# The last 64 rows of the first batch's k and v by one transfer over 128 partitions, and one more spin of TensorE

## The chip, the core and the metric

The kernel runs on one core of a Trainium2 chip. The core has five engines that run their own instruction streams side by side: TensorE (PE, matrix products; PEld is its weight load), VectorE (DVE), ScalarE (ACT), GpSimdE (POOL) and SyncE (SP, which issues most transfers). Transfers between the chip's memory (HBM) and the core's own memory (SBUF, 128 partitions) run on 16 DMA engines, which two queues feed here: one filled by SP, one by ACT. The metric is the device time of one execution in microseconds, lower is better.

## The reference

```python
a = exp(phi - max(phi, axis=2)); a = a / (sum(a, axis=2) + 1e-09)     # phi: 8 batches, 8 heads, 576, 32
k_m = einsum('bhsm,bhsd->bhmd', a, k); v_m = einsum('bhsm,bhsd->bhmd', a, v)
scores = matmul(q, k_m^T) / sqrt(64); scores -= max(scores)
attn = exp(scores) / (sum(exp(scores)) + 1e-09)
x = matmul(attn, v_m)            # laid out as 4608 tokens by 512
h = maximum(x @ w_in, 0); out = (h * h) @ w_out                        # 512 -> 2048 -> 512
```

Everything is in float32. For each batch and head, 576 rows of k and v are reduced to 32 "memories" with the weights exp(phi), queries attend to these 32 memories, and a two-layer feed-forward network with a squared ReLU follows.

## The kernel before, in words

The 576 rows of a batch are five chunks of at most 128 partitions: four full ones and a last one of 64 rows. The eight heads are two groups of four (`qd` 0 and 1). The chunks of phi for both groups stand in `e_sb` (128 partitions, 5 chunks, 256 columns); k and v of one group and chunk are 512 float32 in a partition (4 heads, 64 of k and 64 of v).

The first batch is done before anything else can start, by an order written out by hand (the string `order` that the loop at L1381 follows). Its steps on the path:

- `load_phi` (L161) issues the three transfers of phi: the short last chunk from ACT's queue (L168), the others from SP's (L174, L176).
- `first_kv` (L1302) loads k and v: group 0 from ACT's queue into `u_hi3`, `u_lo3` and `u_hi4`, group 1 from SP's into `wp2` and `wp3`, two chunks by transfer (L1316) and the 64 rows of the last chunk by a transfer of their own (L1320).
- `fetch` (L565) loads the weights `w_in` and `w_out`, 512 KB by transfer, behind these on SP's queue. They come as coded words that ACT, DVE and POOL decode (`decode`, L584 to L609).
- `exp_phi`: DVE takes the maximum over the five chunks (L186, L189), PE and DVE bring it to all rows (L206 to L214), DVE subtracts it (L224), ACT takes the exponential (L225).
- `memories` (L302): PE multiplies each chunk of exponentials with a column of ones (`add`, L318) and with k and v (`product`, L327). Ahead of the products of chunk 2 PE does two products with the identity (L341). DVE and ACT copy the result to `mem` (L417).
- `attend` (L453): scores (L439), their maximum, exponential (L478) and sums. While nothing else is there for it, PE runs `spin`: products with the identity whose result nobody reads (L159).
- `make_u`: PE multiplies the decoded `w_in` (`w_sb`) with the memories (L439, into `ps_m`), and ACT copies this to `u_hi` (L550). The feed-forward products of the first batch (L687, L708) follow.

What sets the order around the change: every engine runs its instructions in program order. Each transfer signals one of eight semaphores, taken in turn by both queues together, and the issue of a transfer waits for the landing of the one that stands eight before it. So at most eight transfers are in flight. ACT's stream has the decode of the first half of `w_in` (L584, L587, L590) between the first exponentials (L225) and its half of the copy of the memories (L417), and the decode of the second half between that copy and the exponentials of the scores (L478). Behind the first batch an instruction plan of fixed places feeds PE with products for the other seven batches.

Of the kernel before, what the change touches and what calls it, by code (L numbers as in the profile page):

```python
# [9 lines left out]
F32 = mybir.dt.float32  # L10
# [17 lines left out]
def attn_moe_kernel(ctx: ExitStack, tc: tile.TileContext, qT, kv, phi, w_in, w_out, outT):  # L28
# [12 lines left out]
    nc = tc.nc  # L41
    ctx.enter_context(tc.manual_schedule())

    B, NQ, S = kv.shape[:3]
    P = 128
# [3 lines left out]
    D = 64  # L49
    M = 32  # L50
# [6 lines left out]
    CW = 2 * D + 2  # L57
    NCH = (S + P - 1) // P
# [9 lines left out]
    def rows(c):  # L68
        return min(P, S - c * P)

    const = ctx.enter_context(tc.tile_pool(name="const", bufs=1))
# [37 lines left out]
    e_sb = const.tile([P, NCH, NQ * P], F32, name="e_sb")  # L109
    kvb = [const.tile([P, 4, CW], F32, name=f"kvb{i}") for i in range(NCH)]  # L110

    def fill(c, t):
        if rows(c) < P:
            nc.gpsimd.memset(t[rows(c):], 0.0)
        if t.shape[-1] == CW:
            nc.gpsimd.memset(t[:rows(c), :, 2 * D:], 1.0)

    def fill_all():
        for c in range(NCH):
            fill(c, kvb[c])  # L120
            if rows(c) < P:
                nc.gpsimd.memset(e_sb[rows(c):, c], 0.0)

    ones = const.tile([P, CW - 2 * D], F32, name="ones")
    nc.gpsimd.memset(ones, 1.0)
# [35 lines left out]
    def load_phi(b, nc_q=nc.sync):  # L161
        nfull = S // P
        assert b == 0 or ("products", b - 1) in ready
        n = nfull if b else nfull // 2
        x = phi[b, :nfull * P].rearrange("(c p) x -> p c x", p=P)
        def short():
            if nfull < NCH:
                nc_q.dma_start(out=e_sb[:rows(nfull), nfull], in_=phi[b, nfull * P:])  # L168
                if b >= 3:
                    nc_q.dma_start(out=e_sb[P - rows(nfull):, nfull], in_=phi[b, nfull * P:])  # L170

        if not b:
            short()
        nc.sync.dma_start(out=e_sb[:, :n], in_=x[:, :n])  # L174
        if not b:
            nc.sync.dma_start(out=e_sb[:, n:nfull], in_=x[:, n:])  # L176
        if b:
            short()
        return [e_sb[:P if b >= 3 else rows(c), c] for c in range(NCH)]

    def chunk_max(e):

# [119 lines left out]
    def memories(b, e, kvs, mem):  # L302
# [9 lines left out]
        accs = [bank(ps, qd if not b or two else 0)[:, (qd if b and not two else 0) * CW:] for qd in range(NQ)]  # L312
        sums = [(ps_h.tile([P, 512], F32, name="h") if qd else tp) if not b else accs[qd][:, 2 * D:] for qd in range(NQ)]

        def add(qd, c):
            n = kvs[qd][c].shape[0]
            for j in range(4):
                nc.tensor.matmul(  # L318
                    sums[qd][M * j:M * (j + 1), :CW - 2 * D], e[c][:n, qd * P + M * j:qd * P + M * (j + 1)], ones[:n],
                    start=(c == 0), stop=(c == len(kvs[qd]) - 1),  # L320
                )

        def product(qd, c):
            y = kvs[qd][c]
            n, w = y.shape[0], y.shape[-1]
            for j in range(4):
                nc.tensor.matmul(  # L327
                    accs[qd][M * j:M * (j + 1), :w],
                    e[c][:n, qd * P + M * j:qd * P + M * (j + 1)],
                    y[:, j, :], start=(c == 0), stop=(c == len(kvs[qd]) - 1),  # L330
                )

# [26 lines left out]
        if two:  # L359
            n = rows(NCH - 1)  # L360
            for j in range(4):
                for qd in range(NQ):
                    y = kvs[qd][-1] if qd else kvs[qd][-1][:n]
# [22 lines left out]
        for qd in turns:  # L386
            x = accs[qd][:, :2 * D].rearrange("p (x d) -> p x d", x=2)[:, :, None, :].broadcast_to([P, 2, 2, D])
# [9 lines left out]
        if b > 2:  # L397
            done_ps(ps)
            for j in range(4):
                if j == 2 or j and b > JOIN:  # L400
                    yield
                for k in range(2):
                    for x in range(2):
                        at = M * (2 * (j % 2) + k)
# [42 lines left out]
            y = rhs[pr // NQ][hs, pr % NQ]  # L447
            nc.tensor.matmul(out[M * pr:M * (pr + 1), :y.shape[-1]], mem[hs, x, pr], y, start=True, stop=True)  # L448

    spins = [2, 3]  # L450
    on_gpsimd = {(0, 0): (), (0, 1): (), (1, 0): (), (1, 1): (2,), (2, 0): (0, 1, 2), (2, 1): (0,)}

    def attend(b, t, q, mem, new_a):  # L453
# [761 lines left out]
    def task_phi(b):  # L1215
        state[b]["phi"] = load_phi(b)
# [81 lines left out]

    st = state[0]
    kvs = [None] * NQ  # L1300

    def first_kv(qd):  # L1302

        if qd:
            x = [const.tile([P, 2, 2, 4, 2 * D], F32, name=f"wp{k}") for k in (2, 3)]
            rooms = [x[0][:, 0], x[0][:, 1], x[1][:, 0]]
        else:
            rooms = [const.tile([P, 2, 4, 2 * D], F32, name=n) for n in ("u_hi3", "u_lo3", "u_hi4")]
        queues = ((nc.scalar, nc.scalar, nc.scalar), (nc.sync, nc.sync, nc.sync))[qd]
        got = []  # L1310
        for t, nc_q in zip(rooms, queues):
            c = len(got)
            n = min(2, S // P - c)
            if n:
                x = kv[0, qd, c * P:(c + n) * P].rearrange("(c p) h x -> p c h x", p=P)
                nc_q.dma_start(out=t[:, :n], in_=x)  # L1316
                got += [t[:, k] for k in range(n)]
            else:
                fill(c, t[:, 0])
                nc_q.dma_start(out=t[:rows(c), 0], in_=kv[0, qd, c * P:])  # L1320
                got.append(t[:, 0])
        kvs[qd] = got

    def first_phi():
        st["phi"] = load_phi(0, nc.scalar)
        fill_all()
# [231 lines left out]
    for k, step in enumerate(steps):  # L1558
        i, b, t, f = step
# [5 lines left out]
        n = f * P // FC  # L1565
# [53 lines left out]
    for j in range(-1, LAST + 1):  # L1619
# [31 lines left out]
        if new:  # L1651
            ffn1_product(u1, j + 1, 1, True)
            ffn1_product(z, j + 1, 2, True)
            x = from_z(j + 1, 2, *(("g_hi", 3) if old else ("r", 2)))
# [19 lines left out]
    n = (B - JOIN) * REST  # L1674
# [23 lines left out]
    last = banks["h"] + [banks["z"], banks["m"]]  # L1698
# [55 lines left out]
```

## Time and profile before

| | |
|---|---|
| median of 3 runs | 696.65 us (696.21 to 697.31) |
| the profiled execution's own time | 695.58 us |
| its span, first to last instruction | 693.5 us |
| PE busy | 682.5 us (98% of the span) |
| DVE, ACT, POOL busy | 480.5, 439.7, 345.0 us |
| bytes moved by transfers | 89.85 MB, mean 130 GB/s |

A profile lists every instruction's start and duration on each engine and every transfer's issue and landing. The share of busy time is a mean over the program; what the first 60 us are bound by is not what the rest is bound by. The granted clock of TensorE is given as a share of 2.4 GHz, so 0.50 is 1.2 GHz. The profiled execution took 2.1 us more than its span, and 1.07 us less than the median of the three runs.

### The profile page before, as it was taken

The page shows a single profiled execution, that of the slowest core. Times are in us where ns is not written, and L with a number is a line of the kernel's source. Part 1 is how long each engine was busy: PE and PEld are TensorE (multiplying, and loading weights), DVE is VectorE, ACT ScalarE, POOL GpSimd, SP SyncE. Part 2 cuts the span into 40 slices and gives each one's busy share as a digit, 9 for nine tenths or more (in the row PEclk, how much of TensorE's full clock was granted, in tenths as well). Part 3 has the DMA queues.
Part 4 walks back from the last instruction along what each step waited for, and adds up shares of the span by engine and source line. Part 5 has one row for each costly group of instructions (what it writes and reads, how often), then busy time and mean ns, then how long its engine had stood idle before and what let it go on. Part 6 is the DMA issues. An engine that isn't in the chain of part 4 may idle for free.

```text
span 693.5 us, 14173 instructions
## 1 busy us (share of the span) xinstructions
PE 682.5 (98%) x5102; PEld 573.8 (83%) x5102; DVE 480.5 (69%) x1132; ACT 439.7 (63%) x1193; POOL 345.0 (50%) x528
## 2 busy tenths in 40 slices
PE   8899999999999999999999999999999999999997
PEld 4367889899998888888888888888888888888897
DVE  3879849455787976788678976788677765564432
ACT  3867798876456675566666665667666575655531
POOL 2200343343367675747575675757585567554200
PEclk9999999999999999999999999999999999999999
DMA  9997352509424642082336243355106110400102
GB/s 304 353 376 263 126 163 60 187 2 268 139 62 147 219 129 100 25 251 86 97 116 210 88 130 122 118 180 151 64 18 211 62 60 4 166 17 1 57 6 46
DMA packets 67846, 89.85 MB, mean 130 GB/s; under 512 B 6848, under 2 KB 56064, under 8 KB 64192
## 3 DMA queue, kind: packets, MB, share of 16 engines
q1 hardware_dynamic: 65888, 87.41, 38.9%
q10 hardware_dynamic: 1888, 1.54, 0.7%
q8 instruction: 40, 0.66, 0.4%
q14 instruction: 30, 0.25, 0.1%
HBM read 75.30 MB, written 13.63 MB: 128 GB/s over the span
## 4 chain that ended last, share of the span: by engine, by line
PE 91%; DMA 6%; DVE 2%; ACT 1%; issue 0%; ACTq 0%; SPq 0%; DVEq 0%
PE acc L1112 39%; PE h L1136 11%; PE acc L716 9%; PE z L1136 8%; PE h L687 6%; PE acc L708 4%; PE h L1704 2%; DMA e_sb<-in_phi 1%; DMA u_lo<-in_kv 1%; PE z L448 1%; PE m L1704 1%; PE z L1704 1%; PE ps_m L439 1%; PE m L327 1%; PE m L448 1%; DMA wp<-in_w_in 1%
## 5 line engine op out<-in xcount | busy, mean ns | idle before, releaser
L1112 PE MATMUL acc<-u_hi,wp 128*128 128x512 f32 x576 | 153.8, 396 | 0.0
L1112 PE MATMUL acc<-u_lo,wp 128*128 128x512 f32 x576 | 140.0, 392 | 0.0
L1112 PEld LDWEIGHTS acc<-u_hi,wp 128*128 128x128 f32 x576 | 101.2, 188 | 25.9 <-issue 11.0
L1112 PEld LDWEIGHTS acc<-u_lo,wp 128*128 128x128 f32 x576 | 105.5, 188 | 20.5
L1160 POOL TENSOR_TENSOR u_hi<-g_lo,u_hi 128x288 fp32r<-128x288 f32 (+1 forms) x76 | 59.2, 779 | 64.1 <-ACT g_lo L1157 44.2
L700 POOL TENSOR_TENSOR g_lo<-g,g_hi 128x288 fp32r<-128x288 f32 x48 | 43.2, 901 | 78.1 <-ACT g_hi L698 51.4
L1016 POOL TENSOR_TENSOR u_lo<-low,u_hi 128x128 fp32r<-128x128 f32 (+1 forms) x116 | 73.2, 636 | 16.6 <-ACT u_hi L1015 16.0
L1015 ACT CAST u_hi<-low 128x256 fp32r<-128x256 f32 (+1 forms) x160 | 52.8, 347 | 23.0 <-POOL low L1027 19.0
L1152 DVE CUSTOM_DVE_ANT_0 g_hi<-h,g_hi 128x288 f32<-128x288 f32 x95 | 42.7, 449 | 24.5 <-ACT g_hi L1183 24.2
L716 PE MATMUL acc<-g_hi,wp 128*128 128x288 f32 x360 | 58.8, 297 | 0.0
L1183 ACT COPY g_hi<-z 128x288 f32<-128x288 f32 x72 | 28.6, 398 | 44.2 <-PE z L1136 36.6
L716 PEld LDWEIGHTS acc<-g_hi,wp 128*128 128x128 f32 x360 | 51.0, 188 | 4.4 <-ACT r L689 1.7
L1155 ACT ACTIVATE u_hi<-g_hi 128x224 fp32r<-128x224 f32 x95 | 39.0, 410 | 21.7 <-DVE g_hi L1152 21.7
L1177 DVE TENSOR_TENSOR g_lo<-h,g 128x288 f32<-128x288 f32 x48 | 21.5, 448 | 34.9 <-ACT g L1173 33.8
L689 ACT ACTIVATE r<-h 128x288 f32<-128x288 f32 x64 | 26.0, 406 | 27.9 <-PE h L687 27.6
L1136 PE MATMUL z<-a_hi,u_hi 128*128 128x288 f32 x120 | 35.3, 294 | 0.0
L1136 PE MATMUL h<-a_lo,u_hi 128*128 128x288 f32 x120 | 34.6, 295 | 0.0
L716 PE MATMUL acc<-g_lo,wp 128*128 128x288 f32 x180 | 34.6, 295 | 0.0
L1178 POOL TENSOR_TENSOR u_lo<-g_lo,u_lo 128x288 fp32r<-128x288 f32 x30 | 25.1, 835 | 18.5 <-DVE g_lo L1177 18.5
L708 PE MATMUL acc<-g_hi,wp 128*128 128x288 f32 x128 | 33.7, 410 | 0.5 <-ACT a_hi L508 0.5
L1136 PE MATMUL h<-w_sb,u_hi 128*128 128x288 f32 x120 | 34.1, 296 | 0.0
L687 PE MATMUL h<-a_hi,u_hi 128*128 128x288 f32 x128 | 30.8, 327 | 1.0 <-DVE a_hi L493 1.0
(374 smaller groups left out, 1778.1 us busy)
## 6 DMA issues: line engine op xcount, KB each, us to landing
w_sb<-w_f SPq DMA_DIRECT2D x24, 1024.0 KB, 5.5
wp<-in_w_in SPq DMA_DIRECT2D x16, 512.0 KB, 8.4
wp<-in_w_out SPq DMA_DIRECT2D x16, 512.0 KB, 7.9
kvb<-in_kv SPq DMA_DIRECT2D x28, 256.0 KB, 7.1
tmp<-in_kv SPq DMA_DIRECT2D x24, 256.0 KB, 5.8
q_sb<-in_q SPq DMA_DIRECT2D x15, 384.0 KB, 4.7
w_f<-w_sb SPq DMA_DIRECT2D x4, 1024.0 KB, 6.4
e_sb<-in_phi SPq DMA_DIRECT2D x7, 512.0 KB, 4.2
```

The lines of the kernel that those rows point to most:

```text
L687: nc.tensor.matmul(h[:, :T], u[:, qd, fs], x[:, qd], start=(i == 0), stop=(i == len(todo) - 1))
L700: nc.gpsimd.tensor_tensor(out=g_lo, in0=g, in1=g_hi.bitcast(F32), op=ALU.subtract)
L708: nc.tensor.matmul(acc[e][:, :T], wo[f][:, e * P:(e + 1) * P], g_hi, start=first, stop=last)
L716: nc.tensor.matmul(acc[e][:, :T], wo[f][:, w, e * P:(e + 1) * P], x, start=first and x is g_hi and w == 0, stop=last and x is g_lo,)
L1015: nc.scalar.copy(hi[:, k], x)
L1016: by(name, p).tensor_tensor(out=lo[:, k], in0=x, in1=hi[:, k].bitcast(F32), op=ALU.subtract)
L1112: nc.tensor.matmul(late_accs[e], wo[f][:, w, e * P:(e + 1) * P], x, start=f == 0 and first, stop=f == NFT - 1 and last,)
L1136: nc.tensor.matmul(out[:, :T], u[:, lhs], a, start=first and not n, stop=n == 2, skip_group_check=not first)
L1152: nc.vector._custom_dve(TENSOR_ADD_SAT, out=x, in0=u[:, :T], in1=x, s0=float("inf"), s1=0.0)
L1155: nc.scalar.square(g_hi, x[:, :n])
L1160: by(f"c{k}", p).tensor_tensor(out=g_lo, in0=g[:, :n], in1=g_hi.bitcast(F32), op=ALU.subtract)
L1183: (nc.vector.tensor_copy if late_on[f"z{k}"] >> pairs[j][1] & 1 else nc.scalar.copy)(x, banks["z"][:, :T])
```

## The change

The 64 rows of the last chunk of k and v of the first batch are now loaded for both groups by one transfer into 128 partitions: group 0 in partitions 0 to 63, group 1 in 64 to 127 (`last`, a part of `wp3`). So that the weights of the products stand in the same partitions, the 64 rows of phi are loaded twice, into the lower and the upper half, by one transfer whose source is repeated. The products of the last chunk take 64 partitions each in place of 128, of which 64 had been zeros; the three memsets that wrote those zeros are gone, and the one that batch 1 needs in `e_sb` is done later. The second number of `spins` goes from 3 to 4.

```diff
     def fill_all():
         for c in range(NCH):
             fill(c, kvb[c])
-            if rows(c) < P:
-                nc.gpsimd.memset(e_sb[rows(c):, c], 0.0)
...
         def short():
-            if nfull < NCH:
+            if nfull < NCH and not b:
+                n = rows(nfull)
+                y = phi[b:b + 1, nfull * P:].broadcast_to([P // n, n, NQ * P])
+                nc_q.dma_start(out=e_sb[:, nfull], in_=y)
+            elif nfull < NCH:
+                if b == 1:
+                    nc.gpsimd.memset(e_sb[rows(nfull):, nfull], 0.0)
                 nc_q.dma_start(out=e_sb[:rows(nfull), nfull], in_=phi[b, nfull * P:])
...
-        return [e_sb[:P if b >= 3 else rows(c), c] for c in range(NCH)]
+        return [e_sb[:P if b >= 3 or not b else rows(c), c] for c in range(NCH)]
...
+        def part(qd, c):
+            n = kvs[qd][c].shape[0]
+            at = P - n if not b and qd else 0
+            return slice(at, at + n)
+
         def add(qd, c):
-            n = kvs[qd][c].shape[0]
+            n = part(qd, c)
...
-    spins = [2, 3]
+    spins = [2, 4]
...
     def first_kv(qd):
 
         if qd:
             x = [const.tile([P, 2, 2, 4, 2 * D], F32, name=f"wp{k}") for k in (2, 3)]
-            rooms = [x[0][:, 0], x[0][:, 1], x[1][:, 0]]
+            rooms = [x[0][:, 0], x[0][:, 1]]
+            last = x[1][:, 0, 0]
...
-            n = min(2, S // P - c)
-            if n:
-                x = kv[0, qd, c * P:(c + n) * P].rearrange("(c p) h x -> p c h x", p=P)
-                nc_q.dma_start(out=t[:, :n], in_=x)
-                got += [t[:, k] for k in range(n)]
-            else:
-                fill(c, t[:, 0])
-                nc_q.dma_start(out=t[:rows(c), 0], in_=kv[0, qd, c * P:])
-                got.append(t[:, 0])
+            nc_q.dma_start(out=t, in_=kv[0, qd, c * P:(c + 2) * P].rearrange("(c p) h x -> p c h x", p=P))
+            got += [t[:, k] for k in range(2)]
         kvs[qd] = got
+        if qd:
+            n = S - 4 * P
+            nc_q.dma_start(out=last, in_=kv[0, :, 4 * P:])
+            ends.extend([last[:n], last[P - n:]])
```

The source of the new transfer of phi counts 2 copies, 64 rows, 256 elements; that of k and v counts 2 groups, 64 rows, 512 elements. Both destinations count 128 partitions. Every other transfer of the first 30 us counts 128 or 64 rows outermost on both sides.

Transfers at the program's start. SP's stream before (L174 and L176 are phi, `wp_108` and `wp_109` k and v of group 1, `wp_114` and `wp_120` coded `w_in`):

```order
L174 DMA e_sb<-in_phi 128x2x256
L176 DMA e_sb<-in_phi 128x2x256
L1316 DMA wp_108<-in_kv 128x2x512 x2
L1320 DMA wp_109<-in_kv 64x512
L565 DMA wp_114<-in_w_in 128x512
L428 DMA q_sb<-in_q 128x2x288 x2
L565 DMA wp_114<-in_w_in 128x512
L565 DMA wp_120<-in_w_in 128x512 x2
```

and after the change:

```order
L178 DMA e_sb<-in_phi 128x2x256
L180 DMA e_sb<-in_phi 128x2x256
L1324 DMA wp_107<-in_kv 128x2x512 x2
L1329 DMA wp_108<-in_kv 128x1x512
L574 DMA wp_112<-in_w_in 128x512
L437 DMA q_sb<-in_q 128x2x288 x2
L574 DMA wp_112<-in_w_in 128x512
L574 DMA wp_118<-in_w_in 128x512 x2
```

The transfer of the last chunk (64x512 before, 128x1x512 now) stands at the same place and is twice as large. Behind it the first `w_in`, the queries `q_sb` and the other weights follow as before. It now is the eighth transfer of both queues, so it waits for no landing, and the first `w_in` waits for the landing of the short phi.

ACT's stream before, its first four transfers:

```order
L168 DMA e_sb<-in_phi 64x256
L1316 DMA u_hi_125<-in_kv 128x2x512
L1316 DMA u_lo_126<-in_kv 128x2x512
L1320 DMA u_hi_127<-in_kv 64x512
```

and after it, from the end of the first decode on (`wp_112` is the first coded `w_in`, `tmp` and `low` hold its decoded parts, `h` the memories):

```order
L599 ACTIVATE low<-wp_112,tiny 128x512
L426 COPY mem<-h 64x256
L593 ACTIVATE tmp<-wp_112 128x512
L596 ACTIVATE low<-wp_112 128x512
L599 ACTIVATE low<-wp_112,tiny 128x512
L487 ACTIVATE st<-st 128x576
L490 COPY mx<-st 128x1
```

The fourth transfer is gone from ACT's stream and the first now writes 128 partitions. The rest is in the order of before: the copy of the memories (L426, L417 before) stands behind the last step of the first decode, and the exponentials of the scores (L487, L478 before) behind the second.

PE's stream, from the scores of the first queries on, before:

```order
L439 MATMUL acc_283<-q_sb,mem 32x288
L439 MATMUL acc_284<-q_sb,mem 32x288
L159 MATMUL h<-ident 128x512 x2
L159 MATMUL h<-ident,mx 128x512 x3
L439 MATMUL ps_m<-w_sb,mem 32x256 x8
```

and after:

```order
L448 MATMUL acc_278<-q_sb,mem 32x288
L448 MATMUL acc_279<-q_sb,mem 32x288
L157 MATMUL h<-ident 128x512 x2
L157 MATMUL h<-ident,mx 128x512 x4
L448 MATMUL ps_m<-w_sb,mem 32x256 x8
```

One product of a spin more (three to four) stands ahead of the products of `w_sb`. In the last chunk's products, ahead of this, only the operands differ.

## Rows read from the trace of the kernel before

**Rows 1.** Cores: span in us, mean granted clock of TensorE.

```profile
core 0: 693.5 us, clock 0.997
```

**Rows 2.** Windows: us, busy us by engine, granted clock, DMA share, GB/s.

```profile
20.00:60.00 40.00, 36.38 (x323) 23.11 (x329) 32.28 (x52) 29.89 (x48) 3.20 (x3) 0.99 1.01 351
60.00:80.00 20.00, 20.00 (x127) 15.80 (x113) 18.10 (x21) 15.87 (x31) 4.15 (x2) 1.00 0.39 132
```

**Rows 3.** Timeline, program start: start us, us, what, idle before and its releaser.

```profile
0.73 0.57 ACTq L168 DMA_DIRECT2D e_sb<-in_phi  x1
...
4.78 1.34 DVE L189 TENSOR_TENSOR phi_mx<-phi_mx,e_sb 128x256 f32<-128x256 f32 x3 [0.58 <-DMA e_sb<-in_phi]
...
8.99 1.73 ACT L225 ACTIVATE e_sb<-e_sb 128x256 f32<-128x256 f32 x5 [4.47 <-DVE e_sb L224]
...
10.87 1.98 PE L341 MATMUL ps_m<-ident 128*128 128x512 f32 x4
...
13.82 0.70 ACT L584 ACTIVATE tmp<-wp 128x512 f32<-128x512 f32 x1 [3.11 <-DMA wp<-in_w_in]
...
14.15 0.40 PE L327 MATMUL acc<-wp,e_sb 128*32 128x128 f32 x8
...
15.16 0.87 ACT L590 ACTIVATE low<-wp,tiny 128x512 f16<-128x512 f32 x1
...
16.71 0.37 ACT L417 COPY mem<-h 64x256 f32<-64x256 f32 x1 [0.67 <-DVE mem L417]
```

**Rows 4.** DMA issues, 0 to 30 us: count, KB each, us to landing.

```profile
wp<-in_w_in SPq DMA_DIRECT2D x5, 512.0 KB, 8.6
...
wp<-in_kv SPq DMA_DIRECT2D x2, 512.0 KB, 8.7
...
e_sb<-in_phi SPq DMA_DIRECT2D x2, 256.0 KB, 3.2
u_hi<-in_kv ACTq DMA_DIRECT2D x1, 512.0 KB, 5.5
u_lo<-in_kv ACTq DMA_DIRECT2D x1, 512.0 KB, 8.6
...
wp<-in_kv SPq DMA_DIRECT2D x1, 128.0 KB, 8.6
...
e_sb<-in_phi ACTq DMA_DIRECT2D x1, 64.0 KB, 3.4
```

**Rows 5.** Windows: all 16 DMA engines early on (last two columns).

```profile
2.00:10.00 8.00, 7.33 (x45) 3.03 (x47) 3.58 (x10) 2.50 (x6) 1.49 (x5) 1.00 1.00 340
10.00:12.00 2.00, 2.00 (x63) 1.51 (x53) 0.27 (x1) 0.72 (x3) 0.00 (x0) 1.00 1.07 248
...
16.00:17.00 1.00, 0.32 (x3) 0.13 (x2) 0.68 (x2) 0.33 (x2) 0.47 (x1) 1.00 1.03 410
```

**Rows 6.** Timeline: scores and exponentials of the first queries.

```profile
17.93 3.48 PE L159 MATMUL h<-ident 128*128 128x512 f32 x4
...
21.46 2.84 PE L159 MATMUL h<-ident,mx 128*128 128x512 f32 x6
...
23.91 1.47 ACT L590 ACTIVATE low<-wp,tiny 128x1024 f16<-128x1024 f32 x1
...
24.23 0.66 PE L439 MATMUL ps_m<-w_sb,mem 64*32 64x256 f32 x16
...
25.40 0.58 ACT L550 COPY u_hi<-ps_m 128x512 f32<-128x512 f32 x1
25.50 1.23 DVE L609 CUSTOM_DVE_ANT_0 w_sb<-tmp,low 128x2048 uint16<-128x2048 uint16 x1 [0.73 <-ACT low L590]
```

**Rows 7.** Windows: TensorE's idle spell and what followed it.

```profile
14.50:17.00 2.50, 1.15 (x10) 0.54 (x6) 2.04 (x6) 1.73 (x4) 0.47 (x1) 1.00 1.03 399
...
18.00:20.00 2.00, 2.00 (x4) 0.97 (x4) 1.90 (x4) 1.97 (x3) 0.00 (x0) 0.50 1.02 408
```

More of the change, by code (lines that the diff above doesn't have):

```diff
@@ L313, in memories @@
         sums = [(ps_h.tile([P, 512], F32, name="h") if qd else tp) if not b else accs[qd][:, 2 * D:] for qd in range(NQ)]
+        def part(qd, c):
+            n = kvs[qd][c].shape[0]
+            at = P - n if not b and qd else 0
+            return slice(at, at + n)
         def add(qd, c):
-            n = kvs[qd][c].shape[0]
+            n = part(qd, c)
             for j in range(4):
                 nc.tensor.matmul(
-                    sums[qd][M * j:M * (j + 1), :CW - 2 * D], e[c][:n, qd * P + M * j:qd * P + M * (j + 1)], ones[:n],
+                    sums[qd][M * j:M * (j + 1), :CW - 2 * D], e[c][n, qd * P + M * j:qd * P + M * (j + 1)], ones[n],
                     start=(c == 0), stop=(c == len(kvs[qd]) - 1),
@@ L324, in product @@
             y = kvs[qd][c]
-            n, w = y.shape[0], y.shape[-1]
+            n, w = part(qd, c), y.shape[-1]
             for j in range(4):
@@ L328, in product @@
                     accs[qd][M * j:M * (j + 1), :w],
-                    e[c][:n, qd * P + M * j:qd * P + M * (j + 1)],
+                    e[c][n, qd * P + M * j:qd * P + M * (j + 1)],
                     y[:, j, :], start=(c == 0), stop=(c == len(kvs[qd]) - 1),
@@ L1300, in attn_moe_kernel @@
     kvs = [None] * NQ
+    ends = []
     def first_kv(qd):
@@ L1305, in first_kv @@
             x = [const.tile([P, 2, 2, 4, 2 * D], F32, name=f"wp{k}") for k in (2, 3)]
-            rooms = [x[0][:, 0], x[0][:, 1], x[1][:, 0]]
-        else:
-            rooms = [const.tile([P, 2, 4, 2 * D], F32, name=n) for n in ("u_hi3", "u_lo3", "u_hi4")]
-        queues = ((nc.scalar, nc.scalar, nc.scalar), (nc.sync, nc.sync, nc.sync))[qd]
+            rooms = [x[0][:, 0], x[0][:, 1]]
+            last = x[1][:, 0, 0]
+        else:
+            rooms = [const.tile([P, 2, 4, 2 * D], F32, name=n) for n in ("u_hi3", "u_lo3")]
+        nc_q = nc.sync if qd else nc.scalar
         got = []
-        for t, nc_q in zip(rooms, queues):
+        for t in rooms:
             c = len(got)
-            n = min(2, S // P - c)
-            if n:
-                x = kv[0, qd, c * P:(c + n) * P].rearrange("(c p) h x -> p c h x", p=P)
-                nc_q.dma_start(out=t[:, :n], in_=x)
-                got += [t[:, k] for k in range(n)]
-            else:
-                fill(c, t[:, 0])
-                nc_q.dma_start(out=t[:rows(c), 0], in_=kv[0, qd, c * P:])
-                got.append(t[:, 0])
-        kvs[qd] = got
+            nc_q.dma_start(out=t, in_=kv[0, qd, c * P:(c + 2) * P].rearrange("(c p) h x -> p c h x", p=P))
+            got += [t[:, k] for k in range(2)]
+        kvs[qd] = got
+        if qd:
+            n = S - 4 * P
+            nc_q.dma_start(out=last, in_=kv[0, :, 4 * P:])
+            ends.extend([last[:n], last[P - n:]])
+        if len(ends) == NQ and kvs[0] and kvs[1]:
+            for q in range(NQ):
+                kvs[q].append(ends[q])
     def first_phi():
```

## Prediction

> **What bounds the kernel now.** I read the cores' row first: one core, 693.5 us, mean clock 0.997 [rows 1]. Then the windows: from 60 us on PE is busy for 20.00 of 20 us, while between 20 and 60 us it lacks 3.6 us of 40 [rows 2]. So whatever moves the start of that full stretch moves the end by as much, and all that the change touches lies in the first 30 us. Third I read the timeline of this start. The reader is to see in it two chains that meet on ACT. One is that of the memories: the maxima on DVE (the third of the three L189 begins at 4.78 + 2/3 of 1.34 = 5.7 us), the exponentials on ACT from 8.99, PE's products with the pair at L341 among them, the last of which ends at 14.15 + 0.40 = 14.55. The other is the decode of the first coded `w_in`: ACT has been idle for 3.11 us when it lands and L584 starts at 13.82, and L590 ends at 15.16 + 0.87 = 16.03. ACT's copy of the memories, L417, stands behind both; it starts at 16.71, released by DVE's copy, so the decode has 0.68 us to spare there [rows 3]. The attention of the first queries, and with it all of the first batch, follows that copy.
>
> Last I read the transfers. Ahead of the first `w_in` (512 KB) stand 64 KB and twice 256 KB of phi, four times 512 KB of k and v, and two last chunks of 128 KB, one on each queue (one of the two rows stands) [rows 4]: 3392 KB, or 212 KB for each of 16 engines. The 16 engines are at work all the time (share 1.00 to 1.07) and move 340 GB/s early and 410 GB/s at best [rows 5], so one engine moves 340/16 = 21.2 to 410/16 = 25.6 GB/s, in the units of rows 4 20.8 to 25.0 KB in a us.
>
> **The change part by part.**
>
> *Work on the engines.* DVE and ACT work on 128 partitions in place of 64 in the last chunk. The five L225, the last of them on 64 partitions, take 1.73 us together, the three L189 1.34 [rows 3], which leaves no room for a 64-partition form at half the time of the others. I take 0; the bounds are 0 and half of one of five, 0.17 us. PE's products of the last chunk are as many as before with 64 partitions each; the products of chunk 4 with 128 take 0.40 us for eight [rows 3], the 64-partition products of `w_sb` 0.66 for sixteen [rows 6]. I take 0, bounds -0.3 and 0.1. The memsets go from POOL, on which nothing of the first 14 us waits; ACT issues one transfer less, some 0.5 us of an engine that then waits for the exponentials anyway: 0. Nothing is queued behind a new wait here.
>
> *The two reshaped transfers.* This is the term that decides. Both sources now count 2 outermost (two copies of phi's rows, two groups of k and v). No transfer of the trace does so: all count 64 or 128, and every such count deals out evenly to 16 engines. At one end of the bounds the new two run on all 16 like the 64-row ones did (64 KB land in 3.4 us, 128 KB in 8.6 beside 512 KB in 8.7 [rows 4], so it is the queue that sets these times): then 64 KB more are 4 KB for each engine, 0.2 us, which the 0.68 us of the decode hide, and the term is 0. At the other end only as many engines work as the outer count has parts, two. Each of these then has 64 KB of phi and 128 KB of k and v beside its sixteenth of the rest, (512 + 2048 + 512)/16 = 192 KB with the first `w_in`: 384 KB in place of 212. I take the second end: I assume that a transfer is dealt out by parts of its outer dimension, with which the 64 rows agree as well as the 128, and two parts make no more than two shares. No row tests that. The Trainium skill, DMA: Bandwidth & Descriptors, says so outright under "Why a DMA increments its semaphore by 16 and not by 1" and "Rules for kernel authors": the engines of a transfer are the largest number up to 16 that divides the outermost count of both sides, and a leading repeat of c copies confines it to c engines. By it the term is the one worked out next, by the nearest rows 0; no run here shows it yet.
>
> Transfers move from about 2 us on. 384 KB take 384/25.0 = 15.4 to 384/20.8 = 18.5 us, so the first `w_in` lands on these two engines at 17.4 to 20.5 us in place of 13.8. The same count for before, 212/20.8 = 10.2 us, gives 12.2, 1.6 early, so the later figure is not too late. I take the middle, 18.9, 5.1 us later than 13.8. ACT's decode then ends at 21.1, past the 16.71 of the copy of the memories: **+4.4 us** (bounds +2.9 and +6.0), and everything behind that copy is as much later.
>
> *What the late phi costs beside it.* The short phi was issued at 0.73 [rows 3] and landed 3.4 us later, at 4.1; with 60 KB more on an engine it lands 2.4 us later alone, 4.8 if a second stream takes every other turn: 6.5 to 8.9. The third maximum wanted it at 5.7, so the exponentials are 0.8 to 3.2 us later, 2.0 in the middle. PE idles in that time, and an idle spell has a price: between 14.5 and 17 us it was busy for 1.15 of 2.5 us, and from 18 to 20 its clock was 0.50, that is 1.2 GHz [rows 7]. At that level two spins took 3.48 us [rows 6] where the pair at L341 took 1.98 [rows 3], 1.5 us more. The memories would end at 14.55 + 2.0 + 1.5 = 18.1 and ACT could copy them 2.2 us later, at 20.2: hidden behind the decode's 21.1. At worst (3.2 and 1.5) it is 21.4, 0.3 us beyond. The last chunk's 128 KB end at 352 KB of an engine, 16.1 to 18.9 us; PE wants them at 13.9 + 2.0 + 1.5 = 17.4 or so, and at their latest they add 0.5 beyond the decode. Without the decode as cover this part would cost 3.5 by itself. The second `w_in` has 68 KB more of each engine ahead of its end (queries and itself), 2.7 us: 21.6, when ACT is just free again at 21.5: 0.1, which I leave out.
>
> *The fourth spin.* Three take 2.84 us, one 0.9. PE's products of `w_sb` wait behind it in PE's stream; they ended at 24.23 + 0.66 = 24.89, and ACT copied them from 25.40, right behind its L590 (23.91 + 1.47 = 25.38); DVE's L609 came at 25.50 [rows 6]. So 0.5 of the 0.9 is hidden by the decode on ACT and **+0.4 us** is left (bounds 0 and 0.9).
>
> *The sum.* 4.4 + 0.4 = 4.8 us: a span of 698.3 and an own time of 695.58 + 4.8 = 700.4. That execution was 1.07 us below the median of the runs, so the median is 696.65 + 4.8 = **701.4 us**, between 699.5 and 703.5 by the bounds. The 3.6 us that PE lacks between 20 and 60 us [rows 2] don't absorb it: they are waits for ACT and DVE, which are as late, and the two engines' queues carry the 172 KB more until the transfers have a pause.
>
> **The rivals.**
>
> *The two transfers run on all 16 engines.* For it: 64-row transfers do. Against it: the outer count. Then only the fourth spin is left, +0.4: 697.05 us, no change. It decides for that as soon as the first `w_in` lands before 14.5.
>
> *The queues gain.* One transfer less stands in the row of eight, and the second `w_in` is issued when the second part of phi has landed and no longer when `u_lo` has; `u_lo` took 8.6 us [rows 4]. At 10 to 12 us the engines move only 248 GB/s in place of 410 [rows 5]; filled up, that is 324 KB or 0.8 us. With 16 engines it gives 695.9 to 696.3. A gain beyond 0.2% has no place in the rows.
>
> *The half clock under the four spins.* If PE's idle spell ahead of the late copy is long enough, the four products run at 0.50 and take as much again, 3.6 us, and the products of `w_sb` wait behind them: 705.0. For it: rows 7. Against it: the two spins ahead of them keep PE busy, and behind two such at half clock the three ran at full clock [rows 6].
>
> **How the numbers follow.** Two engines with the sum above: 0.63. The same with the half clock: 0.14. All 16 engines: 0.17. The queues gain: 0.06. No row decides between two and 16 engines; the count of the new sources makes me weigh it three to one. 0.2% of 696.65 is 1.4 us, about what a measurement of this kernel can tell from no change. Slower by more: 0.61 of the first, 0.14, and 0.02 of the rest, 0.77; within: 0.18; faster: 0.05. The likeliest case alone has 699.5 to 703.5. To leave out no more than 2 in 10, the range takes in part of the 16-engine case and the half clock: 696.7 to 705.2.
>
> **What would show it.** Right: ACT's first `w_in` decode starts at 17 to 21 us after an idle spell of 5 us or more; the third maximum on DVE waits for the short phi; L417 follows the decode at once; the share of the DMA engines falls well below 1 between 5 and 17 us, since 14 of them have little left. Wrong: the first decode still starts near 13.8, and the short phi lands before 5.7. The sum fails in its size if the engines' two queues share otherwise than I assumed, or if later transfers catch up and PE's full stretch begins as early as before.

## The result and the profile after

| | before | after |
|---|---|---|
| median, device time | 696.21 us (5 runs, 694.95 to 697.31) | 702.20 us (5 runs, 701.84 to 703.04) |
| span of the profiled execution | 693.5 us | 699.7 us |
| mean granted clock | 0.997 | 0.990 |

The changed kernel takes 1.0086 times as long, with a 95% interval of 1.0071 to 1.0101: it is slower by 6.0 us, where 4.8 was forecast (a median of 702.2 us, where 701.4 was).

The first view is the timeline of the changed kernel's start: start, duration, engine and line, what is done, and in brackets the idle time ahead of it and what ended that. It answers to [rows 3] and [rows 6]. The lines are 4 to 9 higher than before: L193 was L189, L229 was L225, L336 was L327, L426 was L417, L487 was L478, L559 was L550, L574 was L565, L593 was L584.

```profile
5.97 0.88 DVE L193 TENSOR_TENSOR phi_mx<-phi_mx,e_sb 128x256 f32<-128x256 f32 x2 [2.01 <-DMA e_sb<-in_phi]
9.35 0.35 SPq L574 DMA_DIRECT2D wp<-in_w_in  x1
9.43 0.43 DVE L193 TENSOR_TENSOR phi_mx<-phi_mx,e_sb 128x256 f32<-128x256 f32 x1 [2.57 <-DMA e_sb<-in_phi]
...
12.84 1.74 ACT L229 ACTIVATE e_sb<-e_sb 128x256 f32<-128x256 f32 x5 [8.46 <-DVE e_sb L228]
...
19.68 0.45 PE L336 MATMUL acc<-wp,e_sb 64*32 64x128 f32 x16 [0.67 <-DMA wp<-in_kv]
...
20.78 0.67 ACT L593 ACTIVATE tmp<-wp 128x512 f32<-128x512 f32 x1 [6.21 <-DMA wp<-in_w_in]
...
22.10 0.87 ACT L599 ACTIVATE low<-wp,tiny 128x512 f16<-128x512 f32 x1
22.29 0.41 DVE L426 COPY mem<-h 64x256 f32<-64x256 f32 x1
...
22.75 1.87 PE L448 MATMUL acc<-q_sb,mem 64*32 64x288 f32 x16 [1.21 <-DVE mem L426]
22.99 0.37 ACT L426 COPY mem<-h 64x256 f32<-64x256 f32 x1
...
27.16 0.68 ACT L487 ACTIVATE st<-st 128x576 f32<-128x576 f32 x1 [1.17 <-DVE st L485]
...
32.66 0.59 ACT L559 COPY u_hi<-ps_m 128x512 f32<-128x512 f32 x1 [0.64 <-PE ps_m L448]
```

The reader is to see both chains of [rows 3] late. The third maximum waits for the short phi and begins at 9.43 in place of 5.7, the exponentials at 12.84 in place of 8.99. The first `w_in` lands at 20.8 in place of 13.8, after 6.21 us in which ACT had nothing to do. The decode ends at 22.10 + 0.87 = 22.97 and ACT's copy of the memories stands right behind it at 22.99: 6.28 us late. DVE's copy, the end of the other chain, starts at 22.29. In the kernel before ACT's copy waited for DVE's and started 0.44 us after it (16.27 and 16.71), so by this chain alone it would have come at 22.73: the decode is the later of the two by only 0.24 us. Behind the spins the delay has grown: L559 waits for PE and is 7.26 late (25.40 in [rows 6]). Two lines of the kernel before belong to this, DVE's copy of the memories and PE's scores of the first queries:

```profile
16.27 0.41 DVE L417 COPY mem<-h 64x256 f32<-64x256 f32 x1
...
16.73 1.27 PE L439 MATMUL acc<-q_sb,mem 64*32 64x288 f32 x16 [0.68 <-DVE mem L417]
```

SP's own waits (who waits, for what, us in total, times, longest) show one more link: the first `w_in` was not issued until the short phi had landed.

```profile
SPq L574 <- DMA e_sb<-in_phi: 5.9, 1, 5.9
```

The windows of the same trace answer to [rows 2, 5, 7]:

```profile
core 0: us, PE busy (x) PEld busy (x) DVE busy (x) ACT busy (x) POOL busy (x), PEclk, DMA share, GB/s
5.00:10.00 5.00, 0.85 (x3) 0.09 (x2) 1.28 (x3) 0.00 (x0) 0.00 (x0) 0.80 0.97 347
10.00:12.00 2.00, 1.48 (x6) 1.08 (x7) 0.42 (x1) 0.00 (x0) 0.00 (x0) 0.50 0.98 307
...
14.00:16.00 2.00, 2.00 (x82) 1.94 (x82) 0.12 (x1) 0.57 (x2) 0.00 (x0) 0.81 1.04 319
...
20.00:22.00 2.00, 0.96 (x16) 0.41 (x4) 1.36 (x4) 1.22 (x2) 0.00 (x0) 0.90 1.04 373
...
22.00:28.00 6.00, 5.25 (x20) 1.57 (x20) 3.90 (x9) 4.26 (x9) 1.28 (x1) 0.50 1.01 337
...
40.00:60.00 20.00, 17.87 (x200) 13.30 (x198) 15.27 (x26) 13.39 (x23) 0.00 (x0) 1.00 1.01 371
60.00:80.00 20.00, 20.00 (x133) 14.58 (x132) 18.45 (x25) 14.21 (x26) 3.29 (x2) 1.00 0.56 204
```

From 5 to 10 us PE is busy for 0.85 us, and from 10 to 12 its clock is 0.50, that is 1.2 GHz. From 20 to 22 us it is busy for 0.96 of 2 us, and from 22 to 28 its clock is 0.50 again: the first scores take 1.87 us in place of 1.27. From 60 us on PE is full as before, so the shift should last. It doesn't wholly: three of ACT's instructions in the changed kernel,

```profile
131.52 0.44 ACT L702 ACTIVATE g<-r 128x288 f32<-128x288 f32 x1
...
161.49 0.45 ACT L702 ACTIVATE g<-r 128x288 f32<-128x288 f32 x1
...
252.11 0.63 ACT L797 ACTIVATE e_sb<-e_sb 128x512 f32<-128x512 f32 x1 [1.10 <-DVE e_sb L790]
```

are these in the kernel before:

```profile
124.26 0.45 ACT L693 ACTIVATE g<-r 128x288 f32<-128x288 f32 x1
...
154.63 0.45 ACT L693 ACTIVATE g<-r 128x288 f32<-128x288 f32 x1
...
245.77 0.64 ACT L788 ACTIVATE e_sb<-e_sb 128x512 f32<-128x512 f32 x1 [1.10 <-DVE e_sb L781]
```

The shift is 7.26, 6.86 and 6.34 us: 0.9 us come back between 131 and 252 us.

### The profile page after: what moved, and what is told of

It is laid out like the page before. It is cut to its first block, busy times and chain, and to the rows that moved or that the text cites. A ratio compares the mean times of both kernels' runs of the same rounds, so it can differ in the third digit from the quotient of the medians.

```text
span 699.7 us, 14171 instructions
## 1 busy us (share of the span) xinstructions
PE 684.4 (98%) x5104; PEld 574.7 (82%) x5104; DVE 479.6 (69%) x1132; ACT 439.5 (63%) x1193; POOL 345.2 (49%) x526
## 3 DMA queue, kind: packets, MB, share of 16 engines
q10 hardware_dynamic: 1858, 1.47, 0.7%
## 4 chain that ended last, share of the span: by engine, by line
PE 95%; DMA 3%; DVE 1%; ACT 1%; issue 0%
PE acc L1121 38%; PE h L1145 11%; PE acc L725 10%; PE z L1145 8%; PE h L696 7%; PE acc L717 4%; PE h L1715 2%; DMA wp<-in_w_in 2%; PE ps_m L448 1%; DMA e_sb<-in_phi 1%; PE z L457 1%; PE m L1715 1%; PE z L1715 1%; PE m L336 1%; PE m L457 1%; PE h L157 1%
## 5 line engine op out<-in xcount | busy, mean ns | idle before, releaser
L1121 PEld LDWEIGHTS acc<-u_lo,wp 128*128 128x128 f32 x576 | 105.5, 188 | 20.5
L1187 POOL TENSOR_TENSOR u_lo<-g_lo,u_lo 128x288 fp32r<-128x288 f32 x30 | 25.1, 837 | 18.5 <-DVE g_lo L1186 18.5
```

The costliest lines, as they stand in the source:

```text
L1121: nc.tensor.matmul(late_accs[e], wo[f][:, w, e * P:(e + 1) * P], x, start=f == 0 and first, stop=f == NFT - 1 and last,)
```

## The experiments

The shifts below are against the profiled execution before: first `w_in` decode at 13.82, ACT's copy of the memories at 16.71 [rows 3]. "Above" is the difference of the medians from the kernel before on the same chip (696.21 us for the changed kernel, 695.43 for e1 to e4, 695.59 for e5 to e8, 695.96 for e9 to e12), the ratio is given with its interval. The landings and starts are each from one profiled execution, the times from all runs; e6 and e12, e5 and e11 ran on different chips, each beside the kernel before. In my expectations of e1 and e3 "k" and "v" should read group 0 and group 1; each group holds k and v of four heads. "Last" is the 64-row chunk.

| | short phi | last k and v | spins | first decode | copy | above | ratio |
|---|---|---|---|---|---|---|---|
| after | reshaped | reshaped | 4 | 20.78 | 22.99 | 5.99 | 1.0071 to 1.0101 |
| e1 | 2 of 64 rows | 2 of 64, group 0 ahead of `u_hi` | 4 | 13.86 | 18.66 | 3.19 | 1.0026 to 1.0056 |
| e2 | 2 of 64 | reshaped | 4 | 20.96 | 23.18 | 6.18 | 1.0072 to 1.0100 |
| e3 | reshaped | 2 of 64, group 0 ahead | 4 | 16.01 | 20.96 | 5.45 | 1.0058 to 1.0088 |
| e4 | reshaped | reshaped | 3 | 20.53 | 22.74 | 7.05 | 1.0079 to 1.0106 |
| e5 | 2 of 64 | 2 of 64, as before | 4 | 15.59 | 18.27 | 1.95 | 1.0019 to 1.0042 |
| e6 | reshaped | 2 of 64, as before | 4 | 16.43 | 21.51 | 5.47 | 1.0065 to 1.0091 |
| e7 | 2 of 64 | reshaped, ACT's queue | 4 | 14.04 | 29.02 | 13.25 | 1.0168 to 1.0202 |
| e8 | before | before | 4 | 15.11 | 17.32 | 0.57 | 0.9999 to 1.0019 |
| e9 | 2 of 64 | count 4 | 4 | 17.93 | 20.15 | 2.91 | 1.0025 to 1.0052 |
| e10 | 2 of 64 | count 8 | 4 | 16.99 | 20.24 | 1.65 | 1.0016 to 1.0036 |
| e11 | 2 of 64 | 2 of 64, as before | 3 | 15.53 | 17.74 | 0.90 | 1.0002 to 1.0021 |
| e12 | reshaped | 2 of 64, as before | 4 | 15.93 | 20.27 | 3.19 | 1.0026 to 1.0053 |

**e1, both transfers in two.**

```diff
-                y = phi[b:b + 1, nfull * P:].broadcast_to([P // n, n, NQ * P])
-                nc_q.dma_start(out=e_sb[:, nfull], in_=y)
+                nc_q.dma_start(out=e_sb[:n, nfull], in_=phi[b, nfull * P:])
+                nc_q.dma_start(out=e_sb[P - n:, nfull], in_=phi[b, nfull * P:])
...
-            nc_q.dma_start(out=last, in_=kv[0, :, 4 * P:])
+            nc.scalar.dma_start(out=last[:n], in_=kv[0, 0, 4 * P:])
+            nc_q.dma_start(out=last[P - n:], in_=kv[0, 1, 4 * P:])
```

> The changed kernel with each of its two reshaped transfers issued as two of 64 rows (phi twice on ACT's queue; the last rows of k on ACT's queue, those of v on SP's), the fourth spin kept. If the two outermost parts confined these transfers to two engines, and that alone made the kernel slow: the first coded weights land before 14.5 us, the exponentials start near 9 us, ACT copies the memories within 0.5 us of 16.7, and only the spin is left: 696.6 (0.4 for it, as predicted) to 697.2 (1.0, as the trace of the changed kernel suggests). Rival, that the rest of the change (products of 64 partitions from the upper half, 128-partition exponentials) makes the start late: 701 to 702.

The weights land at 13.86 and the exponentials start at 9.18, as the theory has it. But the copy is 1.95 us late and the median 3.19 above, between the two theories. The timeline shows a cause that I had put in myself: group 0's last rows stand ahead of `u_hi` and `u_lo` on ACT's queue, and PE waits 1.47 us for `u_hi`, until 11.48. (`u_lo`, which my expectation of e5 names beside it, cost PE nothing that shows: its products start at 14.63, when the pair of products with the identity ahead of them ends.)

```profile
11.48 0.43 PE L336 MATMUL acc<-u_hi,e_sb 128*32 128x128 f32 x8 [1.47 <-DMA u_hi<-in_kv]
...
18.66 0.37 ACT L426 COPY mem<-h 64x256 f32<-64x256 f32 x1 [2.60 <-DVE mem L426]
```

**e2, phi in two, k and v reshaped** (the first half of e1's diff).

> The changed kernel with the short phi issued as two transfers of 64 rows; only the last rows of k and v keep the reshaped transfer; four spins. Two engines then carry 328 KB up to the end of the first coded weights, in place of 384 with both and 212 before. Between 13.8 us for 212 and 20.8 for 384 that makes 18.5 us by proportion; the copy of the memories would be 4.0 later than before and the median, with the spin and less the 0.9 that came back later, 699.5 to 700.5. The exponentials should start near 9 us as before. Rival, that the late phi alone makes the start late and the last k and v are hidden: 696.6 to 697.2.

The phi came in time (exponentials at 8.87), and nothing was won: 6.18 above against 5.99 for the whole change. Last rows and weights are as late as there, with 56 KB less on the two engines; the proportion to the KB of an engine, by which I expected 18.5, fails. So does the late phi as the cause of the late weights: here they were issued at 5.27, 9.35 in the changed kernel, and landed no earlier.

```profile
19.94 0.68 PE L336 MATMUL acc<-wp,e_sb 64*32 64x128 f32 x16 [4.92 <-DMA wp<-in_kv]
20.96 0.67 ACT L593 ACTIVATE tmp<-wp 128x512 f32<-128x512 f32 x1 [10.35 <-DMA wp<-in_w_in]
```

**e3, phi reshaped, k and v in two** (the second half of e1's diff).

> The changed kernel with the last rows of k and v issued as two transfers of 64 rows, k on ACT's queue and v on SP's; only the short phi keeps the reshaped transfer; four spins. Two engines then carry 272 KB up to the end of the first coded weights: 16.2 us by proportion, decode done at 18.4. By the prediction, in which the late phi costs 2.0 at the exponentials and 1.5 by the half clock: copy of the memories +3.5, median 699.7 to 700.1. By the trace of the changed kernel, in which the exponentials were 3.85 later and the memories' last products 5.6 later, 0.67 of it for the last k and v: copy +4.5 to +5.3, median 700.3 to 701.3. Rival, that only the coded weights set the start: copy +1.7, median 698.0 to 698.5.

The weights land at 16.01, as by proportion, but don't set the start: the copy waits 2.75 us for DVE's, and is 4.25 late. The median, 5.45 above, lies where the trace of the changed kernel had put it. This run also has e1's order, so e6 repeats it without.

**e4, three spins.**

```diff
-    spins = [2, 4]
+    spins = [2, 3]
```

> The changed kernel with three spins behind the first exponentials in place of four, both reshaped transfers kept. By the prediction the fourth spin costs 0.4: median 0.4 below the changed kernel, 701.8. By the trace of the changed kernel, in which ACT waits 0.64 us for PE's products behind the spins and DVE 1.42: 0.9 to 1.0 below, 701.2 to 701.3. Rival, that nothing waits for the spins: 702.2. The reshaped transfers and the starts up to the copy of the memories stay as they were.

The rival's figure came true in the time: 1.0093 against 1.0086, no gain within the intervals. The trace does show the spin: ACT's copy behind the spins is as late as the exponential ahead of them (26.91 and 31.81 against 20.50 and 25.40 in the kernel before, 6.41 both), where the changed kernel lost 0.60 between the two (6.66 and 7.26). This execution just gave nothing back later; its span is 700.0.

```profile
26.91 0.68 ACT L487 ACTIVATE st<-st 128x576 f32<-128x576 f32 x1 [1.19 <-DVE st L485]
...
31.81 0.58 ACT L559 COPY u_hi<-ps_m 128x512 f32<-128x512 f32 x1
```

**e5, both in two, group 0's last rows behind `u_lo`.**

```diff
-            nc_q.dma_start(out=last, in_=kv[0, :, 4 * P:])
+            nc_q.dma_start(out=last[P - n:], in_=kv[0, 1, 4 * P:])
             ends.extend([last[:n], last[P - n:]])
+        else:
+            nc_q.dma_start(out=ends[0], in_=kv[0, 0, 4 * P:])
```

> The changed kernel with 64-row transfers in place of both reshaped ones, as in e1, but the last rows of group 0 stand at the end of ACT's queue, behind u_lo, as in the kernel before; four spins. In e1 they stood ahead of u_hi and u_lo, and PE waited for these until 14.63 us. If that order was the whole of e1's 1.95 us at the copy of the memories: u_lo lands by 14 us, the copy comes at 16.7 to 17.0, and the median is 0.2 to 0.7 above the kernel before (the second copy of phi and the fourth spin). Rival, that the other halves of the layout (products of 64 partitions, second copy of phi) cost it: the copy still at 18 or later, 2 to 3 us above.

The order was part of e1's loss, not the whole: 1.95 above, at the low end of what the rival gave, with the copy 1.56 late. Some 4 of the change's 6.0 us go away with the two reshaped transfers alone. Most of the 1.56 shows in the trace as PE's wait for `u_hi` and `u_lo`, 1.20 and 0.17 us, though the exponentials start 0.16 earlier than before: `u_hi` now stands behind a second copy of the short phi on ACT's queue and is issued at 1.97 in place of 1.34.

```profile
10.85 0.43 PE L336 MATMUL acc<-u_hi,e_sb 128*32 128x128 f32 x8 [1.20 <-DMA u_hi<-in_kv]
```

**e6, e5 with the reshaped phi.**

> As e5, but with the reshaped transfer of the short phi on: e3 without the order that cost e1 1.95 us. The prediction has the late phi cost 2.0 at the exponentials and 1.5 by the half clock, 3.5 at the copy of the memories, and 0.4 for the spin: median 3.5 to 4.0 above the kernel before. By the coded weights alone, which land at 16 us as in e3 and are decoded by 18.2, it would be 1.5 at the copy and 1.5 to 2.0 in the median. By e3 less e1, 4.25 less 1.95: 2.3 at the copy and 2.5 in the median, if the two delays add up, and up to 4.3 if the later phi hides that order.

5.47 above, more than any theory gave: the late phi alone costs nearly what the whole change costs. The exponentials are 3.79 late, the copy 4.80, and the copy waits for the memories, no longer for the weights. From the first exponential to the copy 8.73 us pass, 7.72 in the kernel before.

```profile
9.38 0.42 DVE L193 TENSOR_TENSOR phi_mx<-phi_mx,e_sb 128x256 f32<-128x256 f32 x1 [2.15 <-DMA e_sb<-in_phi]
...
12.78 1.74 ACT L229 ACTIVATE e_sb<-e_sb 128x256 f32<-128x256 f32 x5 [7.85 <-DVE e_sb L228]
...
21.51 0.37 ACT L426 COPY mem<-h 64x256 f32<-64x256 f32 x1 [2.88 <-DVE mem L426]
```

**e7, e2 with the reshaped k and v at the end of ACT's queue.**

```diff
             ends.extend([last[:n], last[P - n:]])
-            nc_q.dma_start(out=last, in_=kv[0, :, 4 * P:])
+            lasts.append(last)
+        else:
+            nc_q.dma_start(out=lasts[0], in_=kv[0, :, 4 * P:])
```

> e2 (only the last rows of k and v in the reshaped form) with this transfer at the end of ACT's queue in place of SP's. In e2 the first coded weights landed as late as with both reshaped transfers, though the two engines carry 56 KB less. Theory of the queue: each queue is worked off in order on these engines, so the weights wait for the 128 KB that stand ahead of them on SP's queue, whatever ACT's queue carries; with the transfer on ACT's queue the weights land at 14 to 16 us, the last k and v at 17 to 19, the copy of the memories is 3 to 4.5 us later than before and the median 3 to 4.5 above it. Theory of the engine, as in the prediction: what counts is the KB of an engine, 328 as in e2, and the weights land at 19 to 21, the median is 5.5 to 6.2 above the kernel before as in e2.

The weights, issued at 3.78, landed at 14.04, 0.2 later than before and 6.9 earlier than in e2 (issued at 5.27), with the same 328 KB in all for each of the two engines: what stood on ACT's queue didn't hold them up as what stood ahead of them on their own. But the last k and v came far later than either theory had it, at 26, and the kernel lost 13.25 us:

```profile
14.04 0.69 ACT L593 ACTIVATE tmp<-wp 128x512 f32<-128x512 f32 x1 [3.28 <-DMA wp<-in_w_in]
...
26.16 0.68 PE L336 MATMUL acc<-wp,e_sb 64*32 64x128 f32 x16 [11.20 <-DMA wp<-in_kv]
```

SP's queue ran on meanwhile with queries and weights. When the other 14 engines had nothing left, the windows show the two engines alone:

```profile
19.00:20.00 1.00, 0.00 (x0) 0.00 (x0) 0.00 (x0) 0.00 (x0) 0.00 (x0) 0.50 0.62 227
...
22.00:23.00 1.00, 0.00 (x0) 0.00 (x0) 0.00 (x0) 0.00 (x0) 0.00 (x0) 0.50 0.13 49
23.00:24.00 1.00, 0.00 (x0) 0.00 (x0) 0.00 (x0) 0.00 (x0) 0.00 (x0) 0.50 0.13 49
24.00:25.00 1.00, 0.00 (x0) 0.00 (x0) 0.00 (x0) 0.00 (x0) 0.00 (x0) 0.50 0.13 51
```

A share of 0.13 of 16 engines is two, at 25 GB/s each. This is the plainest sight of the confinement in the study. The DMA view of the same trace, from 22 to 25 us, says whose the bytes were (queue: packets, MB, share of 16 engines; q1 is SP's queue, q10 ACT's):

```profile
q1 hardware_dynamic: 26, 0.10, 8.4%
q10 hardware_dynamic: 26, 0.05, 4.4%
```

Both queues had as many packets done on these two engines, and SP's, twice as large, had two thirds of the bytes. So the theory of the queue, by which ACT's queue doesn't matter at all, isn't the whole either: the engines went on with both queues side by side, and that is why the last k and v took until 26.

**e8, the kernel before with four spins** (`spins = [2, 4]`).

> The kernel before with four spins behind the first exponentials in place of three, nothing else. By the prediction ACT's copy of the products behind the spins is 0.4 us later and the median 0.4 above the kernel before. By the changed kernel against its form with three spins, whose copies differ by 0.85 us at 32 us and whose medians don't differ: the copy 0.4 to 0.9 later, and 0 to 0.4 in the median. Rival, that the whole spin of 0.9 us shows: 0.9 in both.

```profile
15.11 0.67 ACT L584 ACTIVATE tmp<-wp 128x512 f32<-128x512 f32 x1 [5.02 <-DMA wp<-in_w_in]
...
21.00 0.68 ACT L478 ACTIVATE st<-st 128x576 f32<-128x576 f32 x1 [0.67 <-DVE st L476]
...
26.36 0.59 ACT L550 COPY u_hi<-ps_m 128x512 f32<-128x512 f32 x1 [0.50 <-PE ps_m L439]
```

L478 is 0.50 late, L550 0.96: the spin shows by 0.46, as predicted, and the median is 0.57 above, with an interval that still holds 0. The first row is a warning: up to it this kernel is the kernel before, and its weights landed 1.3 us later. Single landings scatter by that much between executions.

**e9 and e10, e2 with other counts.**

```diff
-            nc_q.dma_start(out=last, in_=kv[0, :, 4 * P:])
+            nc_q.dma_start(out=last, in_=kv[0, :1, 4 * P:4 * P + 32].broadcast_to([4, 32, 4, 2 * D]))
```

(with 16 rows and a count of 8 in e10). Both leave out most of the last rows: group 0's first 32 or 16 of them are loaded over and over, so the output isn't that of the reference. Bytes, destination and instructions stay.

> e2 with the source of the 256 KB transfer counting 4 outermost in place of 2: rows 512 to 543 of group 0, four times (so the last rows of k and v of both groups are replaced by these; the bytes and the destination stay). If the outermost count is the number of engines, each of four engines carries 264 KB up to the end of the first coded weights, in place of 328 on each of two in e2 and 216 on all in e1 and e5, whose weights landed at 20.9, 13.9 and 15.6 us: by proportion about 17.4, the last k and v at 15 to 17 in place of 19.9, and the median 3 to 4.5 us above the kernel before. Rival, that any source with a leading count that isn't 64 or 128 is on two engines, or is slow for its repeats: weights at 20 to 21, median 5.5 to 6.2 above.

> As e9 with a count of 8: rows 512 to 527 of group 0, eight times. By the outermost count each of eight engines carries 232 KB: weights at 14.5 to 16 us, last k and v before PE wants them at 15, and the median 1.5 to 2.5 us above the kernel before, as in e5. Rival, that the leading count doesn't set the engines: as e2, 5.5 to 6.2 above.

The same 256 KB with a count of 4 land the weights at 17.93 and cost 2.91, with a count of 8 at 16.99 and 1.65, after 20.96 and 6.18 with a count of 2. The outermost count sets it, and repeats as such don't cost. The 17.4 and 14.5 to 16 that I expected were somewhat early, and e9's 2.91 is just below its 3 to 4.5; in e10 the exponentials were also 1.35 late, with no reshaped phi, and the copy waited for the memories, so its start says nothing of the weights. (That execution took 1.1 us more than e10's median.)

**e11, e5 with three spins.**

> e5 (no reshaped transfer, group 0's last rows behind u_lo) with three spins: the changed layout without its two suspected costs. e5 was 1.95 us above the kernel before, and in e8 the fourth spin alone was 0.57 above, of which its trace kept nothing behind 166 us. If the spin is worth 0.4 to 0.6: 1.3 to 1.6 above. If what is left comes from the tenth transfer and the second copy of phi alone: 1.9 above. If the layout itself is free and the executions scatter: 0 to 0.5 above.

0.90 above, between the cases: the changed layout, freed of both, is not faster than before and probably a little slower. The copy behind the spins is as late as the exponential ahead of them (0.94 and 0.91), so the spin shows nothing here, 0.46 in e5. PE waits 0.35 and 0.38 us for `u_hi` and `u_lo`, and ACT's copy is 1.03 late; the decode, whose weights landed at 15.53, and the memories end within 0.1 us of each other there.

**e12, e6 with seven opening spins.**

```diff
-    spin(3, ident)
+    spin(7, ident)
```

> e6 (only the short phi in the reshaped form) with seven spins in place of three at the very start of PE's stream, so that PE is busy until about 9.5 us, when the maxima come, in place of idle from 5.65 to 9.86. In e6 the granted clock was 0.50 from 8 to 14 us and again near 22. By the prediction the half clock costs 1.5 us on the way to the memories: copy at 20.0 and median 1.5 below e6, 4.0 above the kernel before. By e6's trace, in which from the first exponential to the copy only 1.0 us more passes than before: copy at 20.3 to 20.7 and median 0.8 to 1.2 below e6. Rival, that the half clock is hidden: as e6, 5.5 above.

PE is busy through the wait, and its clock stays up. First e6, then e12:

```profile
8.00:10.00 2.00, 0.14 (x1) 0.15 (x2) 0.42 (x1) 0.00 (x0) 0.00 (x0) 0.50 1.04 358
...
12.00:14.00 2.00, 2.00 (x9) 0.49 (x10) 1.68 (x5) 1.23 (x4) 0.00 (x0) 0.50 0.90 261
```

```profile
8.00:10.00 2.00, 2.00 (x6) 0.85 (x5) 0.42 (x1) 0.00 (x0) 0.00 (x0) 1.00 1.02 379
...
12.00:14.00 2.00, 1.85 (x63) 1.07 (x65) 1.73 (x5) 1.56 (x5) 0.00 (x0) 1.00 0.87 280
```

The copy comes at 20.27, 1.24 earlier than in e6. The exponentials were 0.34 earlier already, so 0.9 belongs to the clock on this stretch. The medians differ by 2.3 (5.47 and 3.19 above), more than either expectation, the spans of the two profiles by 1.5; of what lies between 1.24 and 2.3 the traces show no cause.

## Why the prediction was right, and where its sizes were off

**Two engines: right.** e9, e10 and e7's share of 0.13 show it, and undoing it (e5) takes back some 4 us. The Trainium skill's rule on the outermost count (DMA: Bandwidth & Descriptors, "Rules for kernel authors") said the same; the trace agrees, with 20.96, 17.93 and 16.99 us for counts of 2, 4 and 8. The same table there advises one 128-partition transfer in place of two to disjoint halves. Here the two 64-row transfers were the faster ones (1.95 us above the kernel before in e5, 5.99 joined), because the one that joined them counts 2 outermost.

**The first `w_in`: right in kind, too small in size.** Forecast was a landing at 18.9 and +4.4 at the copy (bound 6.0); it was 20.8 and +6.28. The term that was mis-sized is the count of all KB of an engine, over both queues, divided by 20.8 to 25.0 KB a us. e2 (328 KB, 20.96) and e7 (328 KB, 14.04) refute it. What the landings follow more closely is the KB ahead of the weights' end on SP's own queue on the fullest engine: 32 of phi, 64 of k and v, 32 of weights, and the last rows, 128, 64 or 32 KB for counts of 2, 4 and 8, 8 for 64-row transfers, 0 in e7. That makes 256 KB for the changed kernel, e2 and e4 (20.8, 21.0 and 20.5 us), 192 for e9 (17.9), 160 for e10 (17.0), 136 for the kernel before, e1, e5, e8 and e11 (13.8, 13.9, 15.6, 15.1, 15.5), 128 for e7 (14.0). The three with the reshaped phi and 64-row last rows have 136 KB too and come at 15.9 to 16.4 (e12, e3, e6); there the weights are issued only behind the late phi, at 9.6 to 9.9 us. Why 56 KB less on ACT's queue made no difference in e2 stays open; a scatter of 1.3 us is half of what they should have made.

**The late phi: too small, and hidden as forecast.** The short phi was to land at 6.5 to 8.9; the maximum that wanted it began at 9.43, and the exponentials were 3.85 late where 3.2 was the bound. Alone it was to cost 3.5 at the copy; e6 has 4.80. I had also not priced that the first `w_in` is issued only when this phi has landed (5.9 us of SP's wait), though the new order showed it; by e2 it cost the changed kernel nothing. In the changed kernel this chain is 0.24 ahead of the decode (0.9 forecast), so it is hidden there, but barely: with phi in time the kernel is no faster (e2). Nor does mending k and v alone help: e6, whose weights land at 16.4, still costs 5.47. Two chains about equally late stand side by side, and only mending both helps.

**The half clock: about right on the way to the memories, left out behind the copy.** 1.5 was taken for the way to the memories; e12 has 0.9 there, and the copy 1.2 earlier with 0.3 of it from an earlier phi. That part is paid inside the hidden chain. But PE's clock fell a second time while it waited for the late copy, and the scores behind it ran at 0.50 (1.87 us in place of 1.27). From ACT's copy to the exponentials of the scores 4.17 us pass, as in e2, e4 and e9, whose scores ran at 0.50 as well; before it was 3.79, and 3.67 or 3.68 in e1, e5, e8 and e11, whose clock was 1.00 throughout these microseconds. So 0.38 us of the loss is half clock that isn't hidden, and the sum had no term for it. That the four spins would run at half clock didn't come true: eight products took 3.83 us at 28.13.

**The last k and v: hidden, as forecast, but at the edge.** PE waited 0.67 us for them, until 19.7 (bounds 16.1 to 18.9).

**The fourth spin: +0.4, seen as 0.46 in e5 and e8, 0.60 in the changed kernel, 0 with three.** In the time it is worth 0.57 in e8, about 1.0 between e11 and e5, and nothing between e4 and the changed kernel. These agree within their intervals, and no better figure than 0 to 1 follows. (My expectation of e11 has e8's trace keep nothing of the spin late on. It keeps 0.57 of 0.96, of which 0.50 stood there ahead of the spins.)

**Nothing given back: wrong by 0.9.** The shift held from 32 to 131 us; then 0.9 came back. Set against the same execution of the kernel before, nine of the twelve other traces give back 0.2 to 0.8 there, e8, which differs from it by one spin, 0.4; e4, e6 and e12 nothing. Some of it may thus be that one execution's own, and what it is stays open. It offset half of the mis-sized landing, and that the total came within 1.2 us of the forecast is luck to that extent: 6.28 at the copy, 0.38 more at the exponentials of the scores (27.16 against 20.50), the half clock, and 0.60 at the spins, less 0.9, is 6.3 in the trace and 6.0 in the medians, against 4.4 and 0.4.

**The share of the DMA engines below 1: wrong as a sign.** It was 0.97 and 0.98 from 5 to 12 us. So the other 14 engines were at work too; only in e7, where they had run dry, did the share fall.

**Costs taken as 0.** e11 is 0.90 above with neither reshaped transfer nor spin. It has two transfers more than the changed kernel, and its trace shows PE waiting for `u_hi` and `u_lo`. The changed kernel's trace has no such wait, its exponentials being 3.85 late, so nothing shows that this 0.9 is in the change too. No kernel here beat the one before.

## What to carry to other kernels

Before two transfers are joined into one, read the outermost count of both sides: a count of 2 here put 256 KB on two of 16 engines, and the weights queued behind it on the same queue landed some 7 us late. Where two chains meet, price each as if the other were mended; here either alone cost nearly the whole. Where an early load has to be late, keep PE busy through the wait: e12, with four spins more, had its copy 0.9 us earlier by that and was 2.3 us faster than e6 in all.

## What the runs showed of the hardware beside that

- The issue of the doubled phi from ACT took 1.14 us, 0.57 for 64 rows before, though both are one instruction.
- Here a landing depended on what was ahead on its own queue much more than on the other queue's load on the same engines (14.0 and 21.0 us with 328 KB each). Where both queues had work for the same two engines, both got as many packets done (26 each in 3 us of e7), and the one with packets of twice the size had twice the bytes.
- Two engines alone moved 49 to 51 GB/s; 16 moved up to 410 [rows 5], so one engine runs at about 25 GB/s in both.
- The landing of the same transfer in the same place differed by 1.3 us between two executions (13.8 in the kernel before, 15.1 in e8, alike up to there); whether both ran on one chip the record doesn't say.
